# What the loads of one batch wait for: the first or the second half of the previous batch's transposed q

## The chip, the cores and the metric

The kernel runs on one core of one Trainium2 chip. The metric is the device time of one launch in microseconds (us), the median over several runs.

## What is computed

Attention over keys and values that are projected along the sequence, followed by a feed-forward layer. There are 8 batches, 8 heads, 1024 positions, 64 elements a head; the projections E and F reduce 1024 positions to 64.

```python
k_proj = np.einsum('ks,bhsd->bhkd', E, k)
v_proj = np.einsum('ks,bhsd->bhkd', F, v)
scores = (1 / np.sqrt(64)) * np.matmul(q, k_proj.transpose(0, 1, 3, 2))
attn = softmax(scores)                      # over the 64 projected keys
x = np.matmul(attn, v_proj)                 # heads side by side: 8192 x 512
h = x @ w_in                                # 512 -> 2048
out = (h * np.clip(h + 3.0, 0.0, 6.0) / 6.0) @ w_out   # 2048 -> 512
```

Inputs and output are float32. The kernel rounds the inputs to bf16 while it loads them.

## The kernel before

The kernel handles one batch after another, numbered 0 to 7. For each batch the feed-forward layer takes two halves of 512 positions (`t` = 0 and 1). A half has sixteen first groups (`first_group`, lines 522 to 525: four pairs of matmuls with `w_in` into one PSUM tile, then ScalarE and VectorE make the activation `g`) and four second groups (`second_group`, lines 531 to 555: `w_out`, a copy out of PSUM, and a store from SP's queue). The second groups of a half run between the first groups of the next one. The attention of batch b + 1 is fitted between the feed-forward groups of batch b, so TensorE's order is one long list that is written out by hand: nothing reorders it at run time. Small steps that wait for their place are put in the list `later`, and `pop()` (line 609) takes one of them between two groups.

The attention of a batch b >= 1 is the class `Attention` (from line 192):

- `project` (201 to 206) multiplies the raw k and v with E and F on TensorE, in turn for each slice of the sequence, k first and then v.
- `keys_out` and `values_out` (208 to 213) copy the results out of PSUM on VectorE.
- `turn` (216 to 223), a step in `later`, issues transposing DMAs on SP's queue: one of the projected keys into `kT` (line 217), and then, through `q_transposed` (153 to 159), two of the raw q into `qT`. The first of the two covers heads 0 to 3, which are the head pairs j = 0 and 1; the second covers heads 4 to 7, the pairs 2 and 3. `qT` has the layout [128, 4 pairs, 2, 512], so index 0 of its second axis is written by the first DMA, and index `KO // 2` = 2 by the second. (For batch 3, q is transposed at another place, line 704.)
- `turn` ends with a call of `behind_that(last, b + 1, ...)` (185 to 188). GpSimd, which the profile names POOL, copies one element, `last`, into a tile `mark`. POOL executes in order, so the loads that `load_kqv` (116 to 120) issues next on POOL's queue start only when the DMA that writes `last` has landed. These are loads of the raw k, v and q of the next batch, 1 MB each in bf16, read from HBM as float32. The order is k, v, q for batch 2.
- `scores` (226 to 236) multiplies `kT` and `qT` for a pair j; `exps` follows on ScalarE. For batch 1, `visit(0)` (339 to 344) does the pairs 0, 1, 2 in this order, and `visit(1)` does pair 3. For batch 2, `some_scores((2, 0, 1), ...)` (line 691) does pair 2 first.

The raw tiles of k, q and v have two buffers each, so batch 2 uses those of batch 0. The loads of batch 1 are issued at the start, behind the weights (line 134). Only the first element that a DMA writes is needed for a mark: it says that the whole DMA has landed.

The stretch that concerns the change, in TensorE's order: the end of batch 0's feed-forward, the scores of batch 1 among its second groups (lines 628 to 635), the first two groups of batch 1's own feed-forward (683 to 684), the projection of batch 2 (line 689), thirteen more first groups, and the first scores of batch 2 (line 691).

Of the kernel before, what the change touches and what calls it, by code (L numbers as in the profile page):

```python
# [15 lines left out]
def kernel(  # L16
# [19 lines left out]
    KO = d_model // P  # L36
# [116 lines left out]
    def q_transposed(b):  # L153

        t = qT_pool.tile([P, KO, 2, TOK], bf16, tag="qT", name="qT")
        for i in range(2):
            nc.sync.dma_start_transpose(t[:, i * KO // 2:(i + 1) * KO // 2].rearrange("p j a (m n) -> p (j a m) n", n=P),
                                        kqv[b]["q"][:, i * H // 2:(i + 1) * H // 2].rearrange("p h s d -> p (h s d)"))
        return t

    qT_dma = {}
# [23 lines left out]
    def behind_that(last, *what):  # L185
        mark = att.tile([1, 1], bf16, tag="mark", name="mark")
        nc.gpsimd.tensor_copy(mark, last)  # L187
        load_kqv(*what)
# [3 lines left out]
    class Attention:  # L192
# [23 lines left out]
        def turn(self):  # L216
            nc.sync.dma_start_transpose(self.kT, self.kp.rearrange("p h a d -> p (h a d)"))
            last = self.kT[:1, 0, :1]
            if self.b != 3:
                qT_dma[self.b] = q_transposed(self.b)  # L220
                last = qT_dma[self.b][:1, 0, 0, :1]
            if self.b + 1 < B:
                behind_that(last, self.b + 1, "kv" if self.b == 2 else "kvq")

# [513 lines left out]
```

## Time and profile before

| | |
|---|---|
| median of 6 runs | 502.02 us (501.78 to 503.01) |
| the profiled execution: its own time | 502.03 us |
| the profiled execution: span, first to last instruction | 500.2 us |
| granted TensorE clock, mean | 1.000 |
| loads of q by POOL, seven of 1 MB | median 20.2 us from issue to landing |
| q transposes by SP, fourteen | median 5.3 us from issue to landing |
| k transposes by SP, seven | median 6.2 us from issue to landing |

The names of the engines: PE is TensorE's matmul stream and PEld its weight loads, DVE is VectorE, ACT ScalarE, POOL GpSimd and SP SyncE. A row of a timeline has the start in us from the start of the span, the length in us, the engine, the line of the kernel and what was written from what. "SPq" or "POOL ... DMA" rows are the issuing of a DMA, not its movement; a landing is counted from the issue to the moment its semaphore is complete. The chain that ended last is followed back from the last instruction, at each step to what released it; its rows say what set the time of the whole. Times in `mm` are matmuls into one family of PSUM tiles, those in `at` into another.

### The profile page before, as it was taken

What the parts mean: (1) busy time and instruction counts of PE and PEld (TensorE: products, weight loads), DVE (VectorE), ACT (ScalarE), POOL (GpSimd) and SP (SyncE); (2) the same over time, 40 slices, a digit from 0 to 9 for tenths busy, and PEclk for the clock granted to TensorE, in tenths of its full rate; (3) what the DMA queues carried; (4) which work ended last, traced back from release to release, by engine and by line L of the source; (5) the groups of instructions that cost most, each with busy time, mean ns of one, the idle gap of its engine ahead of it and who ended that gap; (6) DMA issues with size and microseconds to landing.
All of it is one profiled execution on the core that took longest, in us unless ns stands there. A gap on an engine that the chain in (4) does not pass through costs nothing.

```text
span 500.2 us, 11181 instructions
## 1 busy us (share of the span) xinstructions
PE 493.8 (99%) x4802; PEld 256.0 (51%) x4802; DVE 285.4 (57%) x438; ACT 239.9 (48%) x414; POOL 39.6 (8%) x60
## 2 busy tenths in 40 slices
PE   8899999999999999999999999999999999999997
PEld 4454554555555545554555555555455545555554
DVE  3581836887559674666648654674755656334420
ACT  3656566665355345433563344643446444343431
POOL 8630020100020020002000020000000000000000
PEclk9999999999999999999999999999999999999999
DMA  9999999896979799549950799209411261101112
GB/s 164 198 202 207 189 172 231 150 175 158 200 132 222 166 202 214 107 118 225 211 114 22 188 191 223 68 26 234 113 43 44 61 175 44 43 23 42 44 43 84
DMA packets 84146, 68.43 MB, mean 137 GB/s; under 512 B 38272, under 2 KB 69760, under 8 KB 84096
## 3 DMA queue, kind: packets, MB, share of 16 engines
q0 software_dynamic: 33008, 29.36, 37.7%
q1 hardware_dynamic: 50864, 37.89, 30.8%
q8 instruction: 37, 0.61, 0.5%
q10 hardware_dynamic: 224, 0.46, 0.3%
q14 instruction: 13, 0.11, 0.1%
HBM read 71.83 MB, written 16.97 MB: 178 GB/s over the span
## 4 chain that ended last, share of the span: by engine, by line
PE 95%; DMA 2%; POOL 2%; issue 0%; DVE 0%; DVEq 0%; POOLq 0%
PE mm L169 89%; PE at L169 2%; DMA v<-in_v_dram 2%; PE mm L253 1%; PE at L232 1%; PE at L253 1%; PE mm L232 1%; POOL q L102 1%; POOL k L106 1%; POOL v L106 0%; PE at L431 0%; PE at L411 0%; PE at L397 0%; PE at L424 0%; DVE o_sb L544 0%
## 5 line engine op out<-in xcount | busy, mean ns | idle before, releaser
L520 DVE SCALAR_TENSOR_TENSOR g<-r,mm 128x512 bf16<-128x512 f32 x256 | 174.6, 687 | 144.2 <-ACT r L519 143.4
L169 PE MATMUL mm<-w_out_sb,g 128*64 128x512 bf16 (+2 forms) x2080 | 235.6, 376 | 0.0
L169 PE MATMUL mm<-xT,w_in_sb 128*64 128x512 bf16 x2048 | 231.1, 379 | 0.0
L519 ACT ACTIVATE r<-mm 128x512 f32<-128x512 f32 x256 | 152.7, 598 | 74.2 <-PE mm L169 73.2
L169 PEld LDWEIGHTS <-w_in_sb 128*64 128x64 bf16 x2048 | 115.9, 110 | 104.7 <-issue 0.6
L169 PEld LDWEIGHTS <-g 128*64 128x64 bf16 x2080 | 114.9, 110 | 106.4 <-issue 7.1
L554 ACT COPY o_sb<-mm 128x512 f32<-128x512 f32 x58 | 34.0, 586 | 149.7 <-PE mm L169 149.3
L273 DVE TRANSPOSE_TENSOR_REDUCE parts<-aT 128x32 f32<-128x1024 bf16 x24 | 28.8, 1226 | 0.0
L265 DVE TENSOR_TENSOR xT<-at,rec 128x512 bf16<-128x512 f32 x32 | 20.5, 682 | 7.2 <-ACT rec L181 5.8
L241 ACT ACTIVATE aT<-at 128x512 bf16<-128x512 f32 x38 | 20.7, 620 | 7.6 <-PE at L232 7.6
L265 DVE TENSOR_TENSOR xT<-mm,rec 128x512 bf16<-128x512 f32 x24 | 15.5, 686 | 7.3 <-PE mm L253 7.2
L187 POOL COPY mark<-qT 1x1 bf16<-1x1 bf16 x5 | 0.9, 178 | 201.6 <-DMA qT<-q 201.6
L210 DVE CAST kp<-at 64x512 bf16<-64x512 f32 x14 | 9.0, 678 | 11.3 <-PE at L169 11.2
L169 PE MATMUL at<-v,f_t 128*64 128x512 bf16 x56 | 13.2, 379 | 0.0
L169 PE MATMUL at<-k,e_t 128*64 128x512 bf16 x56 | 13.2, 379 | 0.0
L241 ACT ACTIVATE aT<-mm 128x512 bf16<-128x512 f32 x18 | 9.7, 604 | 7.1 <-PE mm L232 7.1
L213 DVE CAST vp<-at 64x512 bf16<-64x512 f32 x14 | 9.7, 694 | 0.4
L544 DVE COPY o_sb<-mm 128x128 f32<-128x128 f32 x1 | 0.3, 292 | 16.0 <-PE mm L169 16.0
L169 PEld LDWEIGHTS <-e_t 128*64 128x64 bf16 x56 | 6.2, 110 | 5.7
L89 PE MATMUL mm<-ones 128*128 128x512 bf16 x18 | 6.9, 513 | 1.5 <-DVE ones L82 1.5
L232 PEld LDWEIGHTS <-kT 64*64 64x64 bf16 x224 | 5.6, 106 | 4.5 <-issue 3.5
L509 DVE TENSOR_TENSOR xT<-at,rec 128x512 bf16<-128x512 f32 x4 | 2.5, 684 | 8.2 <-PE at L431 8.2
(69 smaller groups left out, 152.1 us busy)
## 6 DMA issues: line engine op xcount, KB each, us to landing
out_dram<-o_sb SPq DMA_DIRECT2D x63, 256.0 KB, 4.4
rec<-turned_rows SPq DMA_DIRECT2D x48, 256.0 KB, 6.4
k<-in_k_dram POOLq DMA_DIRECT2D x7, 1024.0 KB, 10.1
v<-in_v_dram POOLq DMA_DIRECT2D x7, 1024.0 KB, 15.4
q<-in_q_dram POOLq DMA_DIRECT2D x7, 1024.0 KB, 20.2
w_out_sb<-in_moe_w_out_dram POOLq DMA_DIRECT2D x4, 512.0 KB, 14.8
w_in_sb<-in_moe_w_in_dram POOLq DMA_DIRECT2D x7, 256.0 KB, 9.9
k<-in_k_dram POOLq DMA_DIRECT2D x4, 256.0 KB, 5.7
```

The lines of the kernel that those rows point to most:

```text
L89: nc.tensor.matmul(ps, ones[:, :P], ones, start=True, stop=True)
L169: nc.tensor.matmul(ps[lo:lo + width], stationary[:, lo:lo + width], moving, **flags)
L210: nc.vector.tensor_copy(self.kp[:, :, a, :], self.ps[:KP].rearrange("p (h d) -> p h d", d=D))
L213: nc.vector.tensor_copy(self.vp[a * KP:(a + 1) * KP], self.ps[KP:].rearrange("p (h d) -> p h d", d=D))
L232: nc.tensor.matmul(tiles[r][t * KP:(t + 1) * KP, a * HT:(a + 1) * HT], self.kT[r * D:(r + 1) * D, 2 * j + a, :], qT[r * D:(r + 1) * D, j, ...
L241: when(lambda r=r: nc.scalar.activation(aT[:, :, r, :], tiles[r].rearrange("p (a n) -> p a n", a=2), AF.Exp, scale=scale))
L253: nc.tensor.matmul(tiles[t][c:c + D], stationary(r, 2 * j + a), self.weights(j, a)[r:r + KP], start=True, stop=True)
L265: when(lambda t=t: nc.vector.tensor_mul(self.xT[:, j, t, :], av[t], rec[:, t]))
L273: nc.vector.tensor_reduce(out=self.parts[:, j], op=ALU.add, axis=mybir.AxisListType.X, apply_transpose=True, in_=self.aT[j].rearrange("p a ...
L519: nc.scalar.activation(r, h_ps, AF.Relu, bias=0.5, scale=1.0 / 6.0)
L520: nc.vector.scalar_tensor_tensor(g[:, fo, :], r, 1.0, h_ps, op0=ALU.min, op1=ALU.mult)
L554: (copy or nc.scalar.copy)(o_sb, o_ps)
```

## The change

The element that the mark before batch 2's loads copies is taken from the part of batch 1's `qT` that the second transposing DMA writes. For the other batches the index stays 0. Nothing else is different: the same instructions stand on every engine in the same order.

```diff
@@ -218,7 +218,8 @@
             last = self.kT[:1, 0, :1]
             if self.b != 3:
                 qT_dma[self.b] = q_transposed(self.b)
-                last = qT_dma[self.b][:1, 0, 0, :1]
+
+                last = qT_dma[self.b][:1, KO // 2 if self.b == 1 else 0, 0, :1]
             if self.b + 1 < B:
                 behind_that(last, self.b + 1, "kv" if self.b == 2 else "kvq")
```

## The prediction

> **What bounds the kernel now.** I read the page first: engine totals, then the chain that ended last. TensorE is busy for almost the whole span and the chain is 95% TensorE.
>
> ```profile
> PE 493.8 (99%) x4802; PEld 256.0 (51%) x4802; DVE 285.4 (57%) x438; ACT 239.9 (48%) x414; POOL 39.6 (8%) x60
> ...
> PE 95%; DMA 2%; POOL 2%; issue 0%; DVE 0%; DVEq 0%; POOLq 0%
> ```
>
> Then I read that chain in order of time, around batch 2's attention. Columns: start us, length us, what.
>
> ```profile
> 86.35 1.73 PE at L169 x16
> 88.07 11.22 PE mm L169 x104
> 99.30 0.34 PE mm L232 x8
> 99.64 0.44 PE at L232 x16
> ```
>
> The reader is to see that each piece begins where the last ended: batch 2's k and v are projected from 86.35, 104 feed-forward matmuls follow, and batch 2's first scores start at 99.30. TensorE waits for nobody here. So the change cannot gain much: there is no stall to take away after the first 20 us. It can cost only where a delayed transfer comes later than TensorE asks for it.
>
> Next the POOL and SP timelines of that stretch (start, length, instruction, idle before; SP's in two answers, since a window can merge neighbours), and SP's own waits from 50 to 130 us (total, times, longest):
>
> ```profile
> 67.59 0.18 POOL L187 COPY mark<-qT 1x1 bf16<-1x1 bf16 x1 [36.24 <-DMA qT<-q]
> 68.08 0.87 POOL L120 DMA_DIRECT2D k<-in_k_dram  x1 [0.32 <-issue]
> 68.94 0.88 POOL L120 DMA_DIRECT2D v<-in_v_dram  x1
> 69.81 0.90 POOL L120 DMA_DIRECT2D q<-in_q_dram  x1
> ```
>
> ```profile
> 61.29 1.98 SPq L157 DMA_TRANSPOSE qT<-q  x1
> ```
>
> ```profile
> 63.32 3.85 SPq L157 DMA_TRANSPOSE qT<-q  x1
> ...
> 89.49 1.20 SPq L217 DMA_TRANSPOSE kT<-kp  x1
> 91.26 1.76 SPq L157 DMA_TRANSPOSE qT<-q  x1
> ```
>
> ```profile
> SPq L157 <- DMA q<-in_q_dram: 0.5, 1, 0.5
> ```
>
> POOL's one-element copy (the mark) starts at 67.59 and only then come batch 2's three loads. The last line matters most: SP's transposes of batch 2's q waited 0.5 us for the q load. That load is already the last thing to arrive before batch 2's q can be transposed, so delaying it delays the transposes by the same amount.
>
> **What the Trainium skill says.** "DMA: Bandwidth & Descriptors", section on the anatomy of one SWDGE DMA: a transfer's semaphore fires only after its last byte is confirmed. The trace agrees in kind: the first half of batch 1's qT was issued at 61.29, its landing took 6.2 us (67.49), and the mark began at 67.59. Same page, "Issuing engines are not separate DMA queues": SP's and POOL's transfers share 16 engines and interleave. The trace agrees: from 84 to 86 us POOL's queue moved 0.28 MB and SP's 0.23 MB. "TensorE: Matmul & The Clock Gate", Part 1: the clock falls after an idle window of about 3.4 us. The page of before shows a granted clock of 1.000 and no such gap; a stall of under a microsecond should not reach it.
>
> **The change, part by part.** No instruction is added. One operand moves: the mark for batch 2 reads the second half of batch 1's qT instead of the first.
>
> *The new wait.* The second transpose was issued at 63.32 and landed 5.9 us later: 69.22. With the same 0.1 us from landing to mark, the mark moves from 67.59 to about 69.3, d = 1.7 us. Could the second half land sooner without the load beside it? No: the DMA view by window shows its packets flowing at some 290 GB/s from 67.4 to about 68.7, while the first packets of POOL's queue appear only after 69.5 us, so the two never share the engines. So d is between 1.6 and 1.8.
>
> *What queues behind.* On POOL only the three loads (0.87, 0.88, 0.90 us to issue) and then the next mark, which waits for DMA anyway. SP's stores do not depend on the mark. Batch 1's own scores (68.86 to 69.7) do not either, and DVE, ACT and TensorE never wait on POOL's mark.
>
> *The loads.* Their landing times were 10.0 us for k, 15.4 for v, 21.4 for q: 78.1, 84.3 and 91.2. Moved by 1.7: 79.8, 86.0, 92.9. First user is TensorE, which takes k and v together from 86.2 (the chain says 86.35; I take the earlier). v keeps 0.15 us. Cost zero, but the cover is nearly gone: any slip beyond 1.85 us in v stalls TensorE one for one.
>
> *The transposes of batch 2's q.* SP issues them at 91.26 because q landed at 91.2. The first takes 1.76 us to issue; the second goes at 93.05 and lands 4.9 us later, 97.95. Moved by 1.7: 99.65. The first scores of batch 2 are those of pair 2 (the list is 2, 0, 1), and pairs 2 and 3 are in the second half. They stand in TensorE's queue at 99.30 (99.23 in the timeline). Slack before: 97.95 to 99.30 = 1.35 us (1.28 by the timeline). The delay of 1.7 exceeds it by 0.35 to 0.45. TensorE stands still for about 0.4 us with everything queued behind; since it never idles later, this is not won back.
>
> *After that.* Batch 3's k and v loads start 1.7 us later, at 98.0 for 96.25. They landed after 9.5 and 14.5 us (105.8 and 111.6) and are used at 135.68: over 20 us spare, cost zero. Their tail at 113.3 is still ahead of the reciprocal transfers that SP issues from 115.37.
>
> *Bounds.* Shorter end: the q loads of later batches took 19.9 to 20.4 us to land; if batch 2's takes 20 instead of 21.4, because it meets the stores at other moments, the delay of q is 0.3 and nothing is late: 0. Below zero I exclude for this term, since TensorE has no wait here that could shrink. Longer end: the transposes of k, 64 x 1024 in bf16 = 0.13 MB, now run into the last microsecond of the q load; at about 200 GB/s that is up to 0.65 us more, a stall of 1.05. And the pair of q transposes, 6.7 us from issue to landing here, took 7.9 us for batch 1 (61.29 to 69.22) and 9.4 for batch 4 (175.3 to 184.7). With 7.9 the scores come 1.2 us later still, with 9.4 2.7. I take 0.4: the same pair, with the same neighbours, only moved.
>
> *Sum.* Profiled execution: span 500.2, time 502.03, so 1.83 us around it; the median shown is 502.02, the same. 502.03 + 0.4 = 502.4.
>
> **Rivals.**
> (1) *Hidden*, 502.0: q lands at least 0.4 us faster after issue than in the profile. For it: other batches' 20 us. Against: stores at 72, 77, 81 and 86 us still lie inside the load. It is also the result if the mark already waited for both halves; the trace speaks against that, since the mark started at 67.59, 1.6 us before the second landing.
> (2) *Slower*, 503.6: batch 2's q transposes, moved later, take batch 1's 7.9 us instead of 6.7, beside the tail of the load. The second half lands at 92.95 + 7.9 = 100.85, TensorE waits 1.55 us at the first scores. It decides once the second half is late by more than 2.35 us in all (1.35 of slack, 1.0 that can be measured). For it: the two slower pairs named above. Against: from 91 to 97 in the profile no other queue moves packets, and the moved pair starts when the q load is done, as this one did.
> (3) *Faster*, 501.5: batch 1's second half lands at 69.22 and its user starts at about 69.5, so only 0.3 us is spare; executions where it slips would gain when the loads stay out of the way. Against: no load packet moves before 69.5, and no stall is there in the profile.
>
> **How the numbers follow.** About 0.2% (1.0 us) is what a measurement of this kernel can tell from no change. The forecast, 501.9 to 503.0 around 502.4: 0.60. Hidden, 502.0: 0.17. Slower, 503.6, up to about 505: 0.18. Faster, 501.5 and partly inside the 0.2%: 0.05. Faster than 501.0 gets 0.03, slower than 503.0 gets the 0.18 and 0.02 from the forecast's tail, 0.20, the rest 0.77. For 8 in 10 the range runs from 501.7, below the hidden case by the spread of the runs shown, to 503.7, which takes in the slower case's centre.
>
> **What would show it.** In the changed profile the mark should start at about 69.3 and k's issue at 69.8; v's landing near 86.0 with no wait at the projection; SP's wait for q about 2.2 us instead of 0.5 (0.5 + 1.7); a new TensorE wait at the first L232 scores of batch 2, for DMA, of some 0.4 us; and every later piece of the chain moved by it. Wrong if q lands before 92.5 (hidden), if the pair takes over 7 us (slower), or if TensorE waits at the projection instead.

## The result, and the profile after

The changed kernel takes 502.94 us (19 runs, 502.2 to 504.37) against 501.88 us for the kernel before (39 runs): a ratio of 1.0020, 95% interval 1.0014 to 1.0027. That is 0.7 to 1.4 us more, just at the size that the prediction had set as "no change". The profiled execution took 502.74 us with a span of 500.9, so 0.7 us over the profiled execution of before.

POOL's timeline after, with the same columns as before:

```profile
69.04 0.18 POOL L187 COPY mark<-qT 1x1 bf16<-1x1 bf16 x1 [38.04 <-DMA qT<-q]
69.53 0.87 POOL L120 DMA_DIRECT2D k<-in_k_dram  x1 [0.31 <-PE at L233]
70.39 0.88 POOL L120 DMA_DIRECT2D v<-in_v_dram  x1
71.26 0.90 POOL L120 DMA_DIRECT2D q<-in_q_dram  x1
```

The loads start 1.45 us later. The chain that ended last, in order of time (scores are line 233 here, since the changed kernel has one line more):

```profile
70.39 16.48 DMA v<-in_v_dram
86.88 0.04 issue
86.92 1.89 PE at L169 x15
88.81 11.22 PE mm L169 x104
100.03 0.34 PE mm L233 x8
```

The chain of before went through TensorE without a break here. Now it runs back to the load of v: TensorE has the first matmul of the projection behind it, and waits for v. The scores begin at 100.03 instead of 99.30, and everything after them is 0.7 us later too. TensorE's own waits from 50 to 130 us (engine and line, what it waited for, total, times, longest) are one row, where the kernel before has none, and SP's row for q has grown from 0.5:

```profile
PE at L169 <- DMA v<-in_v_dram: 0.6, 1, 0.6
```

```profile
SPq L157 <- DMA q<-in_q_dram: 1.5, 1, 1.5
```

```profile
90.19 1.21 SPq L217 DMA_TRANSPOSE kT<-kp  x1
92.98 4.29 SPq L157 DMA_TRANSPOSE qT<-q  x2
```

q landed at 92.96 and its transposes followed at 92.98, as forecast. Their second half landed at 99.7 (second issue at 94.8, 4.9 us to landing). Without its wait for v TensorE would have been at the scores at about 99.3, as before (an estimate); with it, it came at 100.03 and found the half ready. So two waits of about the same size lie one behind the other, and this execution shows only the first.

### The profile page after: what moved, and what is told of

The parts are those of the page before. It is cut to its first block, busy times and chain, and to the rows that moved or that the text cites. A ratio compares the mean times of both kernels' runs of the same rounds, so it can differ in the third digit from the quotient of the medians.

```text
span 500.9 us, 11180 instructions
## 1 busy us (share of the span) xinstructions
PE 493.6 (99%) x4802; PEld 258.4 (52%) x4802; DVE 285.3 (57%) x438; ACT 239.9 (48%) x414; POOL 39.6 (8%) x60
## 4 chain that ended last, share of the span: by engine, by line
PE 82%; issue 8%; DMA 7%; POOL 2%; DVE 0%; POOLq 0%; DVEq 0%
PE mm L169 77%; DMA v<-in_v_dram 5%; PE at L169 2%; DMA w_in_sb<-in_moe_w_in_dram 2%; PE mm L254 1%; PE at L233 1%; PE at L254 1%; POOL q L102 1%; PE mm L233 1%; POOL k L106 1%; POOL v L106 0%; POOL q L120 0%; POOL w_in_sb L125 0%; POOL k L120 0%; DVE o_sb L545 0%
## 5 line engine op out<-in xcount | busy, mean ns | idle before, releaser
L169 PEld LDWEIGHTS <-w_in_sb 128*64 128x64 bf16 x2048 | 118.3, 110 | 102.3 <-issue 0.8
L266 DVE TENSOR_TENSOR xT<-mm,rec 128x512 bf16<-128x512 f32 x24 | 15.5, 686 | 7.3 <-PE mm L254 7.2
## 6 DMA issues: line engine op xcount, KB each, us to landing
k<-in_k_dram POOLq DMA_DIRECT2D x7, 1024.0 KB, 10.8
```

The source lines that it names most:

```text
L169: nc.tensor.matmul(ps[lo:lo + width], stationary[:, lo:lo + width], moving, **flags)
L266: when(lambda t=t: nc.vector.tensor_mul(self.xT[:, j, t, :], av[t], rec[:, t]))
```

## The experiments

The theory that I formed from this profile: the change costs what the later of two arrivals costs, v at the projection and the second half of batch 2's q at the scores; a wait at the first hides the second. The rivals: only v's lateness costs; only the scores' wait costs, as predicted; or the cost belongs to waiting for the second half as such and not to the later start of the loads. Except where a run says otherwise its edit is made in the kernel before.

### A second profile of the changed kernel

> The changed kernel once more, for a second profile of it: 502.9, with a TensorE wait of 0.5 to 1.2 us at batch 2's projection for v, and none or a small one (under 0.3 us) at its first scores.

502.97 us, ratio 1.0018 (1.0012 to 1.0025) with 20 runs. The expected wait for v was not there; TensorE's timeline shows the other one:

```profile
100.05 0.41 PE L233 MATMUL mm<-qT,kT 64*64 64x256 bf16 x8 [0.51 <-DVE g L521]
```

In this execution v landed at 86.4, early enough but for some 0.3 us (the first matmul of k starts at 86.13, that of v at 86.43), and the scores waited 0.5 us. The profile puts that down to a VectorE operation that ends at 100.03. The scores do not need that one: in the kernel before they start at 99.23, while VectorE works on the same group until 99.80. But they need the second half of q's transposes, whose issue starts at 95.0 (the pair of transposes, then the times to landing of both):

```profile
L157 SPq DMA_TRANSPOSE qT<-q x2: 1770/2093/2416, 93.2 to 95.0; - x2
...
DMA to landing us min/median/max: 4.4/4.6/4.9
```

The second one takes the 4.9 us and lands at 99.9, and the matmuls follow 0.15 us later (0.13 us in the two profiles below that name this DMA as the releaser). By the timelines the scores start at 99.23 before, at 99.96 in the first profile of after and at 100.05 in this one. So in these two profiles a different wait is seen, and the scores are late by about the same amount.

### The same delay without the second half

```diff
-        nc.gpsimd.tensor_copy(mark, last)
+        for _ in range(8+1 if what[0] == 2 else 1):
+            nc.gpsimd.tensor_copy(mark, last)
```

> The kernel before with its mark on the first half, but eight more one-element POOL copies (0.18 us each and a little between them) ahead of batch 2's loads, so that they start 1.5 to 1.8 us later with nothing else touched. Theory V (only the start of batch 2's loads counts; v lands after TensorE asks for it at the projection): 502.6 to 503.1 us, with a TensorE wait for v of 0.4 to 0.9 us at the projection. Rival H (what costs is tied to the second transpose itself, so a plain delay does nothing): 501.9 and no wait.

503.62 us, ratio 1.0034 (1.0021 to 1.0046). The mark still reads the first half; only the start of the loads moved, to 69.95, 0.4 us later still than in the changed kernel. The loss lies above the expected range. TensorE's timeline at the projection:

```profile
87.80 0.38 PE L169 MATMUL at<-v,f_t 128*64 128x512 bf16 x1 [1.23 <-DMA v<-in_v_dram]
```

The scores follow at 100.84 and wait for nothing: here the second half lands at 100.3, and v's wait is the longer one. A plain delay brings the loss, so it is the start of the loads that costs and not the wait on the second half as such.

### One user later, then both

In the changed kernel, and for a control in the kernel before:

```diff
-                if b == 1 and t == 0 and fo == 1:
+                if b == 1 and t == 0 and fo == 2:
                     second.projected()
```

> The changed kernel with batch 2's projection one feed-forward group later (0.86 us), which gives v and k that much more time; the q load, its transposes and the place of the first scores stay. Theory V: the wait for v goes (16.5 us after its issue it would land 0.15 us ahead); what may then show is the wait of the scores for q's second half that the prediction named, 0.3 to 0.4 us: 502.2 us in all. Rival S (the scores' wait is what costs the whole 1 us): no change, 502.9. If v's lateness varies by more than 0.9 us between executions, a part of the loss stays.

> The control for the run above: the kernel before with the projection one group later. All theories: 501.7 to 502.0 us, as the kernel before, unless that one has small waits for v in some executions, in which case its slower executions (502.5 to 503.0) should become rare.

503.14 us, ratio 1.0024 (1.0015 to 1.0034): no gain, although the wait for v was all but gone (0.2 us from k's first matmul to v's). That is not the expected 502.2 but what the rival "only the scores' wait costs" had named. In the place of v's wait, with the same misleading releaser as above:

```profile
100.04 0.41 PE L233 MATMUL mm<-qT,kT 64*64 64x256 bf16 x8 [0.56 <-DVE g L521]
```

The control took 502.15 us, ratio 1.0002 (0.9994 to 1.0010), so moving the projection costs nothing that can be measured. The rival "only v's lateness costs" falls here. Then both users were moved, again in the changed kernel:

```diff
-                elif b == 1 and t == 0 and fo == 14:
+                elif b == 1 and t == 0 and fo == 15:
                     second.some_scores((2, 0, 1), (*two, more), later.append)
```

> The changed kernel with both users one feed-forward group later: the projection of batch 2 and its first scores (0.86 us more for each). Theory T (two waits lie one behind the other, v at the projection and q's second half at the scores, each of about 0.7 us in a profiled execution, and only the longer counts): both are covered, 501.9 to 502.3. Theory V alone has fallen with the run that moved only the projection (503.1). Rival (the loss is somewhere else, later in the kernel): 502.9 to 503.1 again.

502.33 us, ratio 1.0005 (0.9997 to 1.0013): most of the loss is gone, and what is left cannot be told from zero. Its profile has the first matmul of v at 87.43, some 0.4 us after that of k at 86.99, so a small wait for v is left (v landed at 87.4). Together with the run above this shows that the scores' wait is real and that it is enough for the whole loss. The rival that put the loss later in the kernel falls. Two runs are missing: the changed kernel with only the scores later, which would show what v's wait costs alone, and the kernel before with the scores later, as a control. For v's wait there are the first profile and the eight copies.

### How much delay fits

Four and sixteen copies in place of the eight:

> The kernel before with four more one-element POOL copies instead of eight: the loads start some 0.95 us later than before. Theory T: v had 1.85 us of slack and the scores 1.3, so 0.95 us fit into both if the loads only move; if they also grow by half of what they grew under the full delay (0.5 us), the waits just begin: 501.9 to 502.4. A loss in proportion to the delay without a threshold would be 502.8.

> The kernel before with sixteen more POOL copies: the loads of batch 2 start some 3.8 us later. Theory T: past its slack v stalls TensorE one for one: 84.3 + 3.8 + about 1 us of growth beside the stores is 89.1 against 86.2, a wait of 2.9 us, and the scores, moved by it, wait for nothing: 504.6 to 505.2. If the eight copies' loss (1.6 us) were the whole effect and no slope stood behind it: 503.6.

Four copies: 502.31 us, ratio 1.0004 (0.9996 to 1.0012). Sixteen: 506.52 us, ratio 1.0083 (1.0061 to 1.0105). TensorE's timelines, of four copies and then of sixteen:

```profile
99.92 0.41 PE L233 MATMUL mm<-qT,kT 64*64 64x256 bf16 x8 [0.28 <-DMA qT<-q]
```

```profile
89.06 0.38 PE L169 MATMUL at<-v,f_t 128*64 128x512 bf16 x1 [2.08 <-DMA v<-in_v_dram]
...
102.35 0.41 PE L233 MATMUL mm<-qT,kT 64*64 64x256 bf16 x8 [0.18 <-DMA qT<-q]
```

So there is a threshold and then a slope. The loads' 1.2 us of delay meets the scores' 1.3 us of slack and leaves a small wait there, since q also took 22.1 us and not 21.4; from there on the delay is paid. The sixteen copies cost 4.5 us, more than the expected 504.6 to 505.2. Their profile has a span 4.1 us above that of before, and TensorE's timeline says where it was lost: 0.4 us before the projection (its first matmul at 86.60 instead of 86.18; from 14 to 20 us the granted clock was 0.72, which the copies cannot have caused), 2.5 us at v, 0.2 us at these scores, and 1.0 us more by the first scores of batch 4, which wait 0.8 us for q. Whether the delay causes that last wait is open: the control with the later projection has one of 0.4 us there without any delay.

### Why k and v themselves took longer

v took 15.4 us from issue to landing before and 16.5 after. The four stores of batch 0's second half go out between 72 and 86 us, at times that TensorE sets. Both kernels were run without them, so that these rows of the output are not written:

```diff
-        nc.sync.dma_start(out=o_dst, in_=o_sb)
+        if (b, t) != (0, 1):
+            nc.sync.dma_start(out=o_dst, in_=o_sb)
```

> The changed kernel without the four stores of batch 0's second half (rows 512 to 1023 of the output are not written), which lie inside batch 2's loads. Theory T: 1 MB less shares the engines, so at some 200 GB/s v lands up to 4 us and q up to 5 us earlier, both waits go: 501.8 to 502.1. If the lateness of k and v against the kernel before (10.9 for 10.0 us, 16.5 for 15.4) comes from how the loads meet the stores, it is gone: the same k and v durations as in the next run, within 0.3 us. If it comes from the late start itself, 0.9 us stay.

> The control: the kernel before without the same four stores (rows 512 to 1023 not written). 501.7 to 502.0, as before. Its k and v durations are to be set beside those of the run above.

501.90 us, ratio 1.0000 (0.9992 to 1.0008), and 501.64 us, ratio 0.9993 (0.9985 to 1.0002). The loads of v, in the changed kernel without stores and in the kernel before without stores:

```profile
L120 POOL DMA_DIRECT2D v<-in_v_dram x1: 883/883/883, 70.5 to 70.5; - x1
...
DMA to landing us min/median/max: 13.5/13.5/13.5
```

```profile
L120 POOL DMA_DIRECT2D v<-in_v_dram x1: 883/883/883, 68.6 to 68.6; - x1
...
DMA to landing us min/median/max: 13.5/13.5/13.5
```

The durations are the same to 0.1 us once the stores are out. From issue to landing, in us, by the profiles:

| kernel | k issued | k | v | q | v landed | q landed |
|---|---|---|---|---|---|---|
| before | 68.08 | 10.0 | 15.4 | 21.4 | 84.3 | 91.2 |
| after | 69.53 | 10.9 | 16.5 | 21.7 | 86.9 | 93.0 |
| after, second profile | 69.67 | 10.8 | 15.9 | 21.8 | 86.4 | 93.2 |
| eight copies | 69.95 | 11.6 | 16.9 | 21.9 | 87.7 | 93.6 |
| before, no stores | 67.73 | 9.0 | 13.5 | 17.7 | 82.1 | 87.2 |
| after, no stores | 69.63 | 9.0 | 13.5 | 17.7 | 84.0 | 89.1 |

So what k and v gain in length comes from the stores. The times suggest how: the stores are issued at 72.3, 76.9, 81.3 and 85.6 before, and 0.2 us earlier after; each takes 5 to 7 us to land. So a load that starts later has more of them in its course: the second store is under way from 77 to 83 us, and k lands at 78.1 before and at 80.4 after; the fourth goes out at 85.4 to 85.6, and v lands at 84.3 before and at 86.9 after. The last store has landed by 90.9, before q in both kernels, and q's duration grows by only 0.3 to 0.5 us, while k's and v's grow by 0.5 to 1.6. The start alone does not fix the length: in four profiles with k issued at 69.5 to 69.7, v took 15.9 to 16.9 us, and what makes that spread is not shown.

For q there is a second candidate, which the prediction had named: the transposes of k. They begin to move at 90.5 before, when q has next to no packets left (4 from 90 to 92 us), and at 91 after, beside the last 69 packets of q. The runs without stores cannot tell the two apart, since in both of them q had landed before k's transposes were issued.

### Only q behind the second half

```diff
-            if self.b + 1 < B:
+            if self.b == 1:
+                behind_that(last, 2, "kv")
+                behind_that(qT_dma[1][:1, KO // 2, 0, :1], 2, "q")
+            elif self.b + 1 < B:
```

> Half of the change: k and v of batch 2 wait for the first half of batch 1's transposed q as in the kernel before, and only the load of q waits for the second half, with a mark of its own. Theory T: what counts is when the queue of loads begins, since the three loads fill the engines one after another; q's issue moves by only 0.2 to 0.5 us and its bytes stand behind k and v anyway: 501.9 to 502.2, no wait at either place. If the wait on the second half itself cost something: 502.5 to 502.9.

502.41 us, ratio 1.0005 (0.9996 to 1.0013), a median a little above what was expected. The profile shows no wait of TensorE in this stretch: v landed at 83.95 and q at 90.45, 20.4 us after an issue at 70.05. This execution is also the fastest of the 13. The second mark had nothing to wait for: the second half landed at 68.9, while POOL was still issuing k and v, and q's issue moved by only 0.24 us. So the rule "q behind the second half" costs nothing that can be measured here, because the half has landed by the time q's turn comes.

### The mark taken the other way

```diff
-                last = qT_dma[self.b][:1, 0, 0, :1]
+                if self.b != 1:
+                    last = qT_dma[self.b][:1, 0, 0, :1]
```

> The change in the other direction: batch 2's loads wait only for the transposed keys of batch 1, which land at 62.6 us, so they start some 5 us earlier than in the kernel before and run beside both transposes of batch 1's q. Theory V: v and q of batch 2 are early; no gain over 501.9 since TensorE did not wait. If the loads slow the transposes down by over 0.3 us, TensorE waits at batch 1's scores for pair 2 (69.5 us): 502.5 to 505 us. If not, 501.7 to 501.9.

Batch 2's loads now wait only for the transposed keys of batch 1 and start at 63.18, beside both transposes of batch 1's q. 520.08 us, ratio 1.0359 (1.0345 to 1.0373), far beyond what any theory had named. TensorE waited at batch 1's scores of pair 2:

```profile
85.00 0.64 PE L233 MATMUL at<-qT,kT 64*64 64x256 bf16 x8 [15.54 <-DMA qT<-q]
```

The second transpose took 21.6 us from issue to landing instead of 5.9. The DMA queues from 70 to 80 us in this run (packets, MB, share of 16 engines; q0 is POOL's queue and q1 SP's):

```profile
q0 software_dynamic: 1329, 1.34, 78.9%
q1 hardware_dynamic: 1311, 0.34, 27.0%
```

The reader is to see the two counts: they are nearly equal, as if the queues took turns packet for packet, but the loads' packets are about 1 KB and those of the transpose 256 bytes, so the transpose gets a fifth of the bytes. The rest of the 18 us is TensorE's clock: it was granted at half speed from about 74 us, during the wait, until between 90.5 and 91, so for some 5.7 us of work, which costs half of that, about 2.8 us (an estimate). The mark of the kernel before keeps this loss out.

### A wait that belongs to neither kernel

```diff
-                    (6, 2): lambda: second.some_values((2, 3), two, third)}
+                    (6, 3 if b == 2 else 2): lambda: second.some_values((2, 3), two, third)}
```

> No part of the change: the kernel before with the values of batch 3's last pairs and the first scores of batch 4 a quarter of a second group later (0.86 us). Several profiles show a TensorE wait of 0.4 to 0.7 us there, for batch 4's transposed q, in kernels with and without the change. If that wait makes the slower executions of all of them, this version reaches 501.6 to 501.8 with fewer runs above 502.3; if not, 502.0.

502.00 us, ratio 1.0000 (0.9992 to 1.0008): no gain. The wait for batch 4's q, 0.4 to 0.8 us in four of the profiles, does not make the spread of the runs, or something else takes its place; which of the two is open. No version that writes the whole output is measurably faster than the kernel before.

## Why the prediction was right, and where it was not

- **The mark at 69.3, loads 1.7 us later.** Right: 69.04 and 69.18 in the two profiles, the loads 1.45 and 1.6 us later. In these executions the transposes themselves were issued 0.2 and 0.05 us earlier; counted from their issue the mark moved by 1.65 us in both. The second half landed after 5.9 us, as in the kernel before, so nothing sped it up.
- **q lands at 92.9, its pair of transposes takes 6.7 us.** Right: 92.96 and 93.2, and 6.7 us. SP's wait for q was 2.2 us in the second profile, as forecast; in the first it was 1.5, because there the wait for v delayed the transposes of k too.
- **The scores wait 0.4 us.** The mechanism was right, and its size too small. The scores began 0.73 and 0.82 us later than before. In the second profile that is q's landing, 0.3 us later than the forecast's 92.9 (21.8 us for the load and not 21.4), and 0.1 us from landing to matmul, which I had not counted. The first of these may be the transposes of k, for which the prediction's longer end had up to 0.65 us; no run shows it.
- **v keeps 0.15 us, cost zero.** This step failed. I moved v's landing rigidly with its issue, to 86.0. It landed at 86.9 and 86.4, and the runs without stores show that the stores make the difference. I had named the danger ("any slip beyond 1.85 us in v stalls TensorE one for one") and priced it at nothing. In the first profile the loss appears at this place, but most of it would have come without it: the second half landed at 99.7, 0.4 us after the scores' old time, plus the 0.1 us to the matmul. So v's wait added 0.1 to 0.2 us there and nothing in the second profile (estimates).
- **The sum.** 0.4 us became 1.06 between the medians. The profiles show 0.7 to 0.8 of that. The rest is the spread of executions: the profiled ones lie 0.15 us above the median of before and 0.2 below that of after. What makes an unprofiled execution slower by that much is not shown. The range held by luck in part: 502.94 is 0.06 us below its top, 0.54 us above its centre, and the upper end had been set for slower transposes, not for a late v. It helped that the two waits overlap, so that v's error hardly adds to that of q.
- **The rivals.** "Hidden" fell: q did not come faster. "Slower" named the pair of transposes at 7.9 us; it stayed at 6.7. "Faster" fell; the opposite, loads that run beside the transposes, is what costs 18 us. The clock stayed at 1.000 in the first profile of after, with a longest wait of 0.6 us in this stretch; that is what the page of the Trainium skill that the prediction cites, "TensorE: Matmul & The Clock Gate", Part 1, with its idle window of about 3.4 us, led me to expect.

## What to carry to other kernels

When a transfer is moved, look at every user that it has and at the slack of each; where two slacks are nearly equal, the first wait can hide the second, and curing the one that the profile shows may bring nothing, as moving the projection did here. A transfer that shares the engines with others does not keep its duration when it is moved: allow for the transfers whose times are fixed by other work. A wait that holds back big loads can be worth many times its cost if it keeps a transfer of small packets free: here the mark on the keys, which freed the loads early, cost 18 us.

## What the runs showed of the hardware that I had not expected

In the run with the mark on the keys two DMA queues with work shared the engines by packets and not by bytes: 1329 packets against 1311 in 10 us, 134 GB/s against 34. The Trainium skill, "DMA: Bandwidth & Descriptors", "Queues, rings and completion order", says that each engine goes round its queues packet by packet; the counts agree, if the profile counts as a packet what that page calls one. In the same run the clock of TensorE fell to 0.50 some 4 us into the wait of 15.5 us, and was back at full speed 5.5 to 6 us after the work had begun again.
